# Attention step of a fused kernel: both halves of the next step's scores in one stretch, the mask moved to the end of the step before

## The chip, the cores and the metric

The kernel runs on one core of a Trainium2 chip. The metric is device time in microseconds of one execution; three runs of the kernel before gave a median of 325.79 us (325.31 to 326.69). The trace is of one more, profiled execution.

## The reference, cut to what matters

Three layers run one after another: a linear attention with decay, a mixture of experts with routing that carries over from token to token, and a gated convolution. Only the first is touched. In it, for each block of positions and each head:

```
intra = einsum('bhic,bhjc->bhij', qb, kb) * Dmask[None]      # scores, then mask
intra = einsum('bhij,bhjd->bhid', intra, vb)
inter = einsum('bhid,bhde->bhie', qb * lam_pow[None], kv_state)
out[:, :, sl] = intra + inter
kv_state = lam_block[None, :, None, None] * kv_state + einsum('bhsd,bhse->bhde', kb_dec, vb)
```

The attention's output `x` is then routed: the expert of a token is `argmax(x @ w_gate)` or, where a local gate says so, the expert of the token before; the softmax of the same logits scales the expert's answer.

## The kernel before, in words

The 1536 tokens (2 sequences of 768) are cut into 12 blocks of 128; each is handled for all 8 heads at once. All engines' instructions stand in the order in which the code is written: the whole attention part lies under `tc.manual_schedule` (L526 to L527), so each engine works its own list from first to last, and an instruction that waits holds up all behind it on that engine.

A loop over steps `s` (L553) is a software pipeline over three blocks: at step `s` block `s` gets its mask and scaled queries and keys, block `g1 = s-1` its attention output, block `g2 = s-2` its routing, and block `g3 = s-3` the last parts of routing. The pieces that the prediction follows, with the names of their tiles:

- `scores(g, half)` (L288, matmuls L300): query times key on TensorE, two head pairs to a half, into PSUM tiles `ps`. Its matmuls use 64 rows of the array; most neighbours use 128.
- `mask(g)` (L303, L307): two VectorE multiplications of `ps` by the decay mask, 128x512 each, into `sm`, which `mix(g)` reads (L326, TensorE, into `po`) one step later.
- `mixed(g1)` (L332): ScalarE copies `po` to `xt`; `turned(g1)` (L375, L378, L380): TensorE turns `xt` into token rows and logits, into PSUM tile `rt`.
- `logits(g2)` (L385) and `choice(g2)` (L419 to L421): VectorE takes the maximum `mx` of the logits in `rt`, its index, and the gate `fk`. From `mx` ScalarE makes `nmx` (`shift`, L404), `ex` (`exponents`, L409; it waits for VectorE's L420 as well), then `den` and the copies `xtok` (L391, L393), `softmax(g3)` (L429), then `xt` (L332) and `kp` (`kept`, L440). `kp` waits also for TensorE's `choice_turned` (L436), which reads `fk`.
- `experts(g2)` (L444): VectorE's scan over the tokens, from `kp` into `o_all`; then `keep_state(g1)` (L364, `state`), and at the step's end `keys_rest(s)` (L284, `kd`) and `first_lo` (L202, `wlo`, a weight's low part; from step 4 on). `experts_turned(g2)` (L448) on TensorE waits for `o_all`, and the program makes it wait for `state` too.

Blocks 5 and 11 end a sequence: `keys_rest` is left out at steps 5 and 11, `keep_state` at step 6, since no state follows them.

Of the kernel before, what the change touches and what calls it, by code (L numbers as in the profile page):

```python
# [44 lines left out]
def fused_kernel(ctx, tc, qkv, lam, wgl, w1, w2, wv, cw, wo, out, dbg=None):  # L45
# [148 lines left out]
    def split_hi(w, cs=slice(0, 1024)):  # L194
        if len(w) == 1:
            w.append(w4([P, 1024], F32R, "whi"))
        nc.scalar.copy(w[1][:, cs], w[0][:, cs])  # L197
# [51 lines left out]
    def first(n):  # L249
        return (w1_t if n < 4 else w2_t)[0][n % 4]  # L250

    def first_hi(n, cs=slice(0, 1024)):
        split_hi(first(n), cs)
# [16 lines left out]
    def key_tile(g):  # L270
        if g not in kd_t:
            kd_t[g] = at_p.tile([P, H, D], F32, name="kd", tag="kd")
        return kd_t[g]

    def keys(g, hs=range(HK)):

        if g % NC < NC - 1:
            kd = key_tile(g)
            for h in hs:
                nc.scalar.activation(kd[:, h, :], qk_t[g, 1][:, 0, h * D:(h + 1) * D], AF.Copy, scale=dm[:, h, P - 1:P])  # L280

    def keys_rest(g):
        if g % NC < NC - 1:
            nc.vector.tensor_tensor(  # L284
                key_tile(g)[:, HK:H], qk_t[g, 1][:, 0, HK * D:].rearrange("p (h d) -> p h d", h=H - HK),
                dm[:, HK:H, P - 1:P].to_broadcast([P, H - HK, D]), op=MUL)

    def scores(g, half, early=False):  # L288
        t = qk_t[g, 0]

        if half == 0 and early:
            rt = ps_1.tile([P, 2, HP, P], F32, name="rt", tag="rt")
            ps_t[g] = [rt[:, rh] for rh in range(2)]
        elif half == 0:
            ps_t[g] = [ps_s.tile([P, HP, P], F32, name=f"ps{rh}", tag=f"ps{rh}") for rh in range(2)]
        for hp in (2 * half, 2 * half + 1):
            for rh in range(2):
                r = slice(rh * 64, rh * 64 + 64)
                c0 = (hp % 2) * P
                nc.tensor.matmul(ps_t[g][rh][:, hp, :], t[r, half, 256 + c0:256 + c0 + P], t[r, half, c0:c0 + P],  # L300
                                 start=True, stop=True)

    def mask(g):  # L303
        ps = ps_t.pop(g)
        sm_t[g] = at_p.tile([P, 2, HP, P], F32, name="sm", tag="sm")
        for rh in range(2):
            nc.vector.tensor_tensor(sm_t[g][:, rh], ps[rh], dm[:, rh * HP:(rh + 1) * HP, :], op=MUL)  # L307
# [22 lines left out]
    def mixed(g):  # L330
        xt_t[g] = xt = at_p.tile([P, KD, P], F32, name="xt", tag="xt")
        nc.scalar.copy(xt.rearrange("p (j b) n -> p j b n", b=2),  # L332
                       po_t.pop(g)[:, :, 0:2 * P].rearrange("p b (j n) -> p j b n", j=2))
# [35 lines left out]
    def turned(g, ks=range(KD)):  # L369
        if 0 in ks:  # L370
            rv_t[g] = ps_1.tile([P, 2, 512], F32, name="rt", tag="rt")
        xt, rt = xt_t[g], rv_t[g]
        for k in ks:
            if k < 2:
                nc.tensor.matmul(rt[:, 0, k * P:k * P + XL], xt[:, k, :], wid[:, k, :], start=(k == 0), stop=False,  # L375
                                 skip_group_check=True)
            else:
                nc.tensor.matmul(rt[:, 0, P:XL], xt[:, k, :], wgl_sb[:, k, :], start=False, stop=(k == KD - 1),  # L378
                                 skip_group_check=True)
                nc.tensor.transpose(rt[:, 1, (k - 2) * P:(k - 1) * P], xt[:, k, :], ident)  # L380
# [21 lines left out]
    def shift(g):  # L402
        nmx_t[g] = nmx = at_p.tile([P, 1], F32, name="nmx", tag="nmx")
        nc.scalar.mul(nmx, lg_t[g][1][:, 0:1], -1.0)  # L404
# [117 lines left out]
    def warm(n):  # L522
        for _ in range(n):
            nc.tensor.matmul(pidx, warm_sb[:, 0:P], warm_sb, start=True, stop=True, skip_group_check=True)

    order_a = {mybir.EngineType.PE, mybir.EngineType.DVE, mybir.EngineType.Activation, mybir.EngineType.Pool, mybir.EngineType.SP}  # L526
    with tc.manual_schedule(engines=order_a):  # L527
        warm(10)
        scores(0, 0)
        scores(0, 1)  # L530
        warm(6)
        mask(0)
        keys(0)
        load_qk(3)
        load_qk(4)
        scores(1, 0, True)
        scores(1, 1, True)
        mix_state(0)
        mix(0, 0)
        mix(0, 1)  # L540
        mixed(0)
        mask(1)
        keys_rest(0)
        powers()
        next_state(0)
        warm(2)
        keep_state(0)
        queries(1)
        keys(1)
        keys_rest(1)  # L550
        scores(2, 0)
        turned(0)
        for s in range(2, NT):  # L553
            g1, g2, g3 = s - 1, s - 2, s - 3
            last = s == NT - 1
            if s < NT - 3:
                load_qk(s + 3)
            if s in (2, 4, 6, 8):
                load_next()
            if s in (9, 10):  # L560
                load_next(2)
            scores(s, 1)
            logits(g2)
            choice(g2)
            if last:
                ranks(g3)
                index_factors(g3)
            mask(s)
            decay(g1)
            shift(g2)  # L570
            exponents(g2)
            token_rows(g2)
            if 0 <= g3 < ET - 1:
                softmax(g3)
            if g3 >= 0 and not last:
                ranks(g3)
                index_factors(g3)
            mix_state(g1)
            mix(g1, 0)
            mix(g1, 1)  # L580
            mixed(g1)
            if last:
                counted_rest(g3)
                indices(g3)
                early_fetch()
            next_state(g1)
            choice_turned(g2, g1)
            inverse(g2)
            queries(s)
            kept(g2)  # L590
            if 3 <= s < 11:
                first_hi((s - 3) // 2, HALF[(s - 3) % 2])
            keys(s, range(2))
            experts(g2)
            keep_state(g1)
            if not last:
                scores(s + 1, 0)
            turned(g1, (0, 1))
            if last:
                turned(g1, (2, 3))  # L600
            experts_turned(g2)
            if not last:
                turned(g1, (2, 3))
            if last:
                softmax(g2)
                parts_hi(g2)
                first_hi(4, HALF[0])
            one_hots(g2)
            if last:
                first_hi(4, HALF[1])  # L610
            keys_rest(s)
            keys(s, range(2, HK))
            if s == NT - 2:
                softmax(g2)
            if s >= 4:
                first_lo((s - 4) // 2, HALF[s % 2])
            if g3 >= 0 and not last:
                counted_rest(g3)
                indices(g3)
            counted(g2)  # L620

        ge, g0, g1 = NT - 3, NT - 2, NT - 1
        logits(g0)
        choice(g0)
        shift(g0)
        exponents(g0)
        token_rows(g0)
        mix_state(g1)
        mix(g1, 0)
        mix(g1, 1)  # L630
        ranks(ge)
        places(ge)
        parts_lo(ge)
        mixed(g1)
        choice_turned(g0, g1)
        kept(g0)
        place(ge, (0,))
        first_lo(4, HALF[0])
        experts(g0)
        inverse(g0)  # L640
        parts_hi(g0)
        turned(g1, (0, 1))
        experts_turned(g0)
        turned(g1, (2, 3))
        one_hots(g0)
        counted_rest(ge)
        counted(g0)
        softmax(g0)
        load_next(4)
        load64(0)  # L650
        first_lo(4, HALF[1])
        place(ge, (1,))
        logits(g1)
        choice(g1)
        token_rows(g1)
        ranks(g0)
        places(g0)
        early_turn(0, (0, 1))
        choice_turned(g1, NT)
        early_turn(0, (2, 3))  # L660
        kept(g1)
        parts_hi(g1)
        experts(g1)
        parts_lo(g0)
        place(g0, (0,))
        experts_turned(g1)
        one_hots(g1)
        shift(g1)
        exponents(g1)
        counted_rest(g0)  # L670
        counted(g1)
        place(g0, (1,))
        ranks(g1)
        places(g1)
        inverse(g1)
        softmax(g1)
        parts_lo(g1)
        early_turn(1, (0, 1, 2, 3))
        place(g1)
        early_split()  # L680
        index_factors(ge)
        index_factors(g0)
        index_factors(g1)
# [3 lines left out]
    last = keep.tile([P, 2], F32, name="last")  # L687
# [657 lines left out]
```

## Time and profile before

| what | value |
|---|---|
| median of 3 runs | 325.79 us |
| the profiled execution's own time | 326.86 us |
| its span, first to last instruction | 325.1 us |
| attention: start of step 2's scores to the first expert matmul | 13.25 to 73.67 us of the span |
| TensorE busy, whole span | 315.7 us, 97% |
| VectorE, ScalarE busy, whole span | 259.0 us (80%), 208.6 us (64%) |
| granted TensorE clock, mean of the span | 0.997 |

PE is TensorE's matmuls, PEld its weight loads, DVE VectorE, ACT ScalarE. The matmuls' ends are modelled, and they overlap; what a group costs its engine is read from start to start. The same holds for VectorE and ScalarE, where an instruction's start lies a little before the end of the one ahead. An execution's time is the span and what lies around it.

### The profile page before, as it was taken

How to read it: one execution, taken by the hardware profiler on the slowest of the kernel's cores; microseconds unless marked ns; L12 is line 12 of the kernel's file. 1: busy time of each engine (PE TensorE's matmuls, PEld its weight loads, DVE VectorE, ACT ScalarE, POOL GpSimd, SP SyncE). 2: the span in 40 equal slices, each digit the busy share in tenths (PEclk: the TensorE clock that was granted, in tenths of full speed). 3: DMA queues.
4: the chain of work that ended last, by engine and by line, in shares of the span. 5: the costliest groups of instructions: out<-in, count | busy, mean ns of one | idle time of the engine just before them, and what ended most of it. 6: DMA issues, size and time to landing. Idle time of an engine off the chain costs nothing.

```text
span 325.1 us, 7326 instructions
## 1 busy us (share of the span) xinstructions
PE 315.7 (97%) x2722; PEld 277.2 (85%) x2722; DVE 259.0 (80%) x561; ACT 208.6 (64%) x518; POOL 91.5 (28%) x113
## 2 busy tenths in 40 slices
PE   8899999999999999999999999999999989999994
PEld 3688888789879899899798897988988969989984
DVE  5688899976958969959799798795845897977970
ACT  1589799966637756576567665864655774764641
POOL 7000000200445640541535405534332441020000
PEclk9999999999999999999999999999999999999998
DMA  7999899366679789589498697993303131331112
GB/s 213 390 389 310 289 375 323 131 209 242 197 251 374 299 287 357 216 315 351 171 343 346 193 398 300 314 386 112 102 34 111 36 98 69 100 94 66 66 42 95
DMA packets 27399, 73.09 MB, mean 225 GB/s; under 512 B 3798, under 2 KB 8156, under 8 KB 27356
## 3 DMA queue, kind: packets, MB, share of 16 engines
q1 hardware_dynamic: 24612, 64.83, 55.2%
q0 software_dynamic: 2304, 7.42, 7.4%
q8 instruction: 25, 0.41, 0.5%
q10 hardware_dynamic: 440, 0.30, 0.3%
q14 instruction: 18, 0.15, 0.1%
HBM read 57.79 MB, written 14.73 MB: 223 GB/s over the span
## 4 chain that ended last, share of the span: by engine, by line
PE 88%; DMA 5%; ACT 2%; DVE 2%; issue 1%; SPq 1%; POOL 0%; POOLq 0%; ACTq 0%
PE ph L854 27%; PE py L868 19%; PE py L1039 10%; PE pv L1013 7%; PE py L878 5%; PE ps L300 4%; PE po L326 3%; DMA qk<-in_qkv_dram 2%; PE rt L375 2%; PE po L318 2%; DMA yg<-ys,yslot 2%; DMA ys<-yo 1%; PE px L827 1%; PE sp L355 1%; PE rt L378 1%; PE rt L380 1%
## 5 line engine op out<-in xcount | busy, mean ns | idle before, releaser
L202 DVE TENSOR_TENSOR wlo<-wraw,whi 128x1024 fp32r<-128x1024 f32 (+1 forms) x69 | 83.4, 1235 | 12.9 <-ACT whi L197 12.9
L854 PE MATMUL ph<-xh,whi 128*128 128x240 f32 x512 | 87.0, 276 | 0.2 <-ACT xh L519 0.2
L854 PEld LDWEIGHTS ph<-xh,whi 128*128 128x128 f32 x512 | 77.4, 189 | 2.2 <-issue 1.2
L854 PE MATMUL ph<-xh,wlo 128*128 128x240 f32 x256 | 70.0, 275 | 0.0
L197 ACT CAST whi<-wraw 128x1024 fp32r<-128x1024 f32 (+1 forms) x69 | 65.6, 990 | 1.1 <-DVE wlo L202 1.0
L868 PE MATMUL py<-whi,hh 128*128 128x512 f32 x176 | 57.2, 396 | 0.0
L854 PEld LDWEIGHTS ph<-xh,wlo 128*128 128x128 f32 x256 | 48.5, 190 | 0.0
L999 DVE SCALAR_TENSOR_TENSOR gt<-yt,cw_sb,gt 128x256 f32<-128x256 f32 x96 | 39.0, 479 | 1.1 <-ACT gt L991 1.1
L868 PEld LDWEIGHTS py<-whi,hh 128*128 128x128 f32 x176 | 33.0, 188 | 7.4
L857 ACT ACTIVATE hh<-ph 128x480 fp32r<-128x480 f32 x32 | 18.3, 573 | 32.0 <-PE ph L854 31.7
L226 POOL TENSOR_TENSOR f64a<-f64a,f64s 128x512 f32<-128x512 f32 (+1 forms) x9 | 20.6, 2285 | 55.1 <-DVE f64s L225 55.0
L1013 PEld LDWEIGHTS pv<-yh,wv_t 128*128 128x128 f32 x288 | 35.2, 192 | 0.7 <-ACT gt L991 0.4
L1013 PE MATMUL pv<-yh,wv_t 128*128 128x256 f32 x288 | 35.7, 284 | 0.0
L868 PE MATMUL py<-wlo,hh 128*128 128x512 f32 x88 | 34.7, 395 | 0.0
L1039 PE MATMUL py<-wo_t,gh 128*128 128x512 f32 (+1 forms) x156 | 34.0, 375 | 0.0
L1039 PEld LDWEIGHTS py<-wo_t,gh 128*128 128x128 f32 x156 | 27.4, 188 | 5.0
L859 DVE SCALAR_TENSOR_TENSOR hh<-ph,hh 128x480 fp32r<-128x480 f32 x32 | 20.9, 653 | 9.3 <-ACT hf L858 9.3
L807 POOL DMA_INDIRECT xr<-xd,idx x14 | 19.6, 1398 | 9.9 <-DVE wlo L202 6.8
L957 POOL DMA_INDIRECT yg<-ys,yslot x8 | 11.4, 1422 | 30.2 <-PE pt L967 20.9
L868 PEld LDWEIGHTS py<-wlo,hh 128*128 128x128 f32 x88 | 16.5, 188 | 3.5
L878 PE MATMUL py<-wraw,hf 128*64 128x256 f32 x160 | 18.4, 382 | 0.0
L491 POOL DMA_INDIRECT xr<-xd,idx x2 | 2.1, 1054 | 52.0 <-ACT kp L440 51.7
(198 smaller groups left out, 520.2 us busy)
## 6 DMA issues: line engine op xcount, KB each, us to landing
wraw<-in_w_dram SPq DMA_DIRECT2D x64, 512.0 KB, 6.5
qk<-in_qkv_dram SPq DMA_DIRECT2D x23, 512.0 KB, 7.9
ys<-yo SPq DMA_DIRECT2D x16, 256.0 KB, 2.2
ys<-warm_sb SPq DMA_DIRECT2D x24, 128.0 KB, 1.9
xd<-xtok SPq DMA_DIRECT2D x11, 260.0 KB, 3.9
out_dram<-oo SPq DMA_DIRECT2D x11, 256.0 KB, 2.0
wraw<-in_w_val_dram SPq DMA_DIRECT2D x4, 512.0 KB, 8.3
wraw<-in_w_out_dram SPq DMA_DIRECT2D x4, 512.0 KB, 8.9
```

The costliest lines, as they stand in the source:

```text
L197: nc.scalar.copy(w[1][:, cs], w[0][:, cs])
L202: nc.vector.tensor_tensor(w[2][:, cs], w[0][:, cs], w[1][:, cs].bitcast(F32), op=SUB)
L226: nc.gpsimd.tensor_tensor(a.bitcast(F32), a.bitcast(F32), s.bitcast(F32), op=ADD)
L807: nc.gpsimd.indirect_dma_start(xr[:, t, :], None, xd, bass.IndirectOffsetOnAxis(ap=idx[:, 2 * e + t:2 * e + t + 1], axis=0))
L854: nc.tensor.matmul(ph[:, fi, :], w1_t[e][k][1 + a][:, f * P:(f + 1) * P], xh[b][:, k].rearrange("p t n -> p (t n)")[:, 0:C1], start=first, ...
L857: nc.scalar.activation(hh[:, 0, :, 0:C1], ph, AF.Relu)
L859: nc.vector.scalar_tensor_tensor(hh[:, 1, :, 0:C1], ph, 0.0, hh[:, 0, :, 0:C1].bitcast(F32), op0=ALU.max, op1=SUB)
L868: nc.tensor.matmul(py, hhs[f // 2][:, a, f % 2, t * P:(t + 1) * P], w2_t[e][f // 2][1 + b][:, (f % 2) * DM:(f % 2 + 1) * DM], start=(n == ...
L878: nc.tensor.matmul(py[i * NW:(i + 1) * NW, 0:DM // 2], hf[:, f, :], w2_t[e][f // 2][0][:, (f % 2) * DM + i * DM // 2:(f % 2) * DM + (i + 1 ...
L999: nc.vector.scalar_tensor_tensor(gt[:, k, :], yt_t[b, k][:, c0 + j:c0 + j + 256], cw_sb[:, k, j:j + 1], gt[:, k, :], op0=MUL, op1=ADD)
L1013: nc.tensor.matmul(pv[:, mi, :], wv_t[:, a, k * DM + m * P:k * DM + (m + 1) * P], yh[b][:, k, :], start=first, stop=last)
L1039: nc.tensor.matmul(po, gh[a][:, k, t * P:(t + 1) * P], wo_t[:, b, k * DM + cs.start:k * DM + cs.stop], start=(i == 0), stop=(i == 11))
```

## The change

The second half of `scores` no longer stands at the start of step `s` but behind the first half, at the end of the step before; eight short matmuls follow each other where four stood twice. `mask(s)` no longer stands behind `choice(g2)` in step `s` but as `mask(s+1)` at the end of step `s`, after `one_hots(g2)` and ahead of `keys_rest(s)` and `keys(s, ...)`. The first of them goes ahead of the loop. No instruction is added or removed, and none on ScalarE, GpSimd or the DMA queues changes its place.

```diff
--- before.py
+++ after.py
@@ -549,7 +549,9 @@
         keys(1)
         keys_rest(1)
         scores(2, 0)
+        scores(2, 1)
         turned(0)
+        mask(2)
         for s in range(2, NT):
             g1, g2, g3 = s - 1, s - 2, s - 3
             last = s == NT - 1
@@ -559,13 +561,11 @@
                 load_next()
             if s in (9, 10):
                 load_next(2)
-            scores(s, 1)
             logits(g2)
             choice(g2)
             if last:
                 ranks(g3)
                 index_factors(g3)
-            mask(s)
             decay(g1)
             shift(g2)
             exponents(g2)
@@ -595,6 +595,7 @@
             keep_state(g1)
             if not last:
                 scores(s + 1, 0)
+                scores(s + 1, 1)
             turned(g1, (0, 1))
             if last:
                 turned(g1, (2, 3))
@@ -608,6 +609,8 @@
             one_hots(g2)
             if last:
                 first_hi(4, HALF[1])
+            if not last:
+                mask(s + 1)
             keys_rest(s)
             keys(s, range(2, HK))
             if s == NT - 2:
```

VectorE, the end of step 8 and the start of step 9, before (the number behind a name is the tile's, `ps_958` the scores of block 9; `mx` belongs to block 7):

```order
L444 SCALAR_TENSOR_TENSOR o_all<-kp,sp 8x128
L364 TENSOR_TENSOR state<-sdec,sp 128x256
L284 TENSOR_TENSOR kd<-qk_598,dm 128x256
L202 TENSOR_TENSOR wlo<-wraw,whi 128x512
L385 MAX mx<-rt 128x8
L419 MAX_INDEX mi<-mx,rt 128x8
L420 TENSOR_SCALAR fk_136<-rt,thr 128x8
L421 SCALAR_TENSOR_TENSOR fk_136<-iota_133,mi,fk_136 128x8
L307 TENSOR_TENSOR sm<-ps_958,dm 128x512
L307 TENSOR_TENSOR sm<-ps_959,dm 128x512
L467 SCALAR_TENSOR_TENSOR scr,rk<-pidx,soall 128x8
```

and of the changed kernel, the same stretch:

```order
L444 SCALAR_TENSOR_TENSOR o_all<-kp,sp 8x128
L364 TENSOR_TENSOR state<-sdec,sp 128x256
L307 TENSOR_TENSOR sm<-ps_958,dm 128x512
L307 TENSOR_TENSOR sm<-ps_959,dm 128x512
L284 TENSOR_TENSOR kd<-qk_605,dm 128x256
L202 TENSOR_TENSOR wlo<-wraw,whi 128x512
L385 MAX mx<-rt 128x8
L419 MAX_INDEX mi<-mx,rt 128x8
L420 TENSOR_SCALAR fk_136<-rt,thr 128x8
L421 SCALAR_TENSOR_TENSOR fk_136<-iota_133,mi,fk_136 128x8
L467 SCALAR_TENSOR_TENSOR scr,rk<-pidx,soall 128x8
```

The two rows `sm` for block 9 stood behind `fk`; now they stand between `state` and `kd`, ahead of `mx`.

TensorE, the end of step 9 from the second row of `choice_turned` on, before (`ps_1064` are the scores of block 10):

```order
L436 MATMUL sp<-ident_100,fk_136 64x128
L300 MATMUL ps_1064<-qk_785 128x128
L300 MATMUL ps_1065<-qk_785 128x128
L300 MATMUL ps_1064<-qk_785 128x128
L300 MATMUL ps_1065<-qk_785 128x128
L375 MATMUL rt<-wid,xt 128x137 x2
L448 LDWEIGHTS o_all
L448 MATMUL sp<-ident_100,o_all 128x8
```

and of the changed kernel:

```order
L436 MATMUL sp<-ident_100,fk_136 64x128
L300 MATMUL ps_1064<-qk_792 128x128
L300 MATMUL ps_1065<-qk_792 128x128
L300 MATMUL ps_1064<-qk_792 128x128
L300 MATMUL ps_1065<-qk_792 128x128
L300 MATMUL ps_1064<-qk_792 128x128
L300 MATMUL ps_1065<-qk_792 128x128
L300 MATMUL ps_1064<-qk_792 128x128
L300 MATMUL ps_1065<-qk_792 128x128
L375 MATMUL rt<-wid,xt 128x137 x2
L448 LDWEIGHTS o_all
L448 MATMUL sp<-ident_100,o_all 128x8
```

The second four rows L300 of block 10 came after `turned` and the counting matmuls L460, ahead of L318; now they follow the first four at once.

## Rows read from the trace of the kernel before

**Rows 1.** The page, part 4: share of the chain that ended last, by engine.

```profile
PE 88%; DMA 5%; ACT 2%; DVE 2%; issue 1%; SPq 1%; POOL 0%; POOLq 0%; ACTq 0%
```

**Rows 2.** Windows; busy time (instructions) of each engine, granted clock, DMA share, GB/s.

```profile
9.00:13.25 4.25, 3.55 (x50) 2.72 (x51) 2.95 (x8) 2.59 (x9) 0.33 (x2) 1.00 0.99 391
52.23:57.21 4.98, 4.98 (x83) 4.32 (x85) 4.69 (x17) 4.83 (x22) 0.00 (x0) 1.00 0.84 292
28.04:62.47 34.43, 34.17 (x539) 29.57 (x539) 31.73 (x110) 31.34 (x138) 0.00 (x0) 1.00 0.84 297
```

**Rows 3.** Timeline of ScalarE; start us, us, engine, line, op, out<-in.

```profile
28.04 0.26 ACT L440 ACTIVATE kp<-sp 8x128 f32<-8x128 f32 x1
...
37.88 0.26 ACT L440 ACTIVATE kp<-sp 8x128 f32<-8x128 f32 x1
...
41.97 0.26 ACT L440 ACTIVATE kp<-sp 8x128 f32<-8x128 f32 x1
...
47.29 0.26 ACT L440 ACTIVATE kp<-sp 8x128 f32<-8x128 f32 x1
...
52.23 0.26 ACT L440 ACTIVATE kp<-sp 8x128 f32<-8x128 f32 x1
...
55.30 0.20 ACT L404 ACTIVATE nmx<-mx 128x1 f32<-128x1 f32 x1
55.53 0.27 ACT L409 ACTIVATE ex<-rt,nmx 128x8 f32<-128x8 f32 x1
...
56.75 0.58 ACT L332 COPY xt<-po 128x512 f32<-128x512 f32 x1
57.21 0.26 ACT L440 ACTIVATE kp<-sp 8x128 f32<-8x128 f32 x1
...
62.47 0.27 ACT L440 ACTIVATE kp<-sp 8x128 f32<-8x128 f32 x1
```

**Rows 4.** Timeline of VectorE, steps 9 and 10.

```profile
52.53 0.47 DVE L444 TENSOR_TENSOR_SCAN o_all<-kp,o_all,sp 8x128 f16<-8x128 f32 x1 [0.17 <-ACT kp L440]
52.92 0.38 DVE L364 TENSOR_TENSOR state<-sdec,sp 128x256 f32<-128x256 f32 x1
53.24 0.40 DVE L284 TENSOR_TENSOR kd<-qk,dm 128x256 f32<-128x256 f32 x1
53.57 0.67 DVE L202 TENSOR_TENSOR wlo<-wraw,whi 128x512 fp32r<-128x512 f32 x1
54.26 0.17 DVE L385 MAX8 mx<-rt 128x8 f32<-128x8 f32 x1
...
55.01 1.28 DVE L307 TENSOR_TENSOR sm<-ps,dm 128x512 f32<-128x512 f32 x2
56.21 0.16 DVE L467 SCALAR_TENSOR_TENSOR scr<-pidx,soall 128x8 f32<-128x8 f32 x1
```

**Rows 5.** Timeline of all engines, one place where `ex` waited.

```profile
39.59 0.17 DVE L385 MAX8 mx<-rt 128x8 f32<-128x8 f32 x1
...
39.96 0.21 DVE L420 TENSOR_SCALAR fk<-rt,thr 128x8 f16<-128x8 f32 x1
...
40.29 0.27 ACT L409 ACTIVATE ex<-rt,nmx 128x8 f32<-128x8 f32 x1 [0.28 <-PE ps L300]
```

**Rows 6.** Timeline of TensorE, three places.

```profile
9.09 1.16 PE L300 MATMUL rt<-qk 64*128 64x128 f32 x16 [0.85 <-DMA qk<-in_qkv_dram]
...
29.94 0.17 PE L460 MATMUL pidx<-so,upto 128*128 128x8 f16 x1
30.03 0.71 PE L300 MATMUL ps<-qk 64*128 64x128 f32 x8
30.68 0.67 PE L318 MATMUL po<-qs,state 64*64 64x128 f32 x16
...
64.07 0.17 PE L460 MATMUL pidx<-so,upto 128*128 128x8 f16 x1 [0.28 <-ACT soall L454]
64.17 0.67 PE L318 MATMUL po<-qs,state 64*64 64x128 f32 x16
```

## The prediction

> **What bounds the kernel now.** I read the page's chain of waits first: 88% of it is TensorE [rows 1]. That speaks for a matmul-bound kernel, but it is a share of the whole span, and the change lies in the attention steps alone. So next I read one full step by windows, from one `kp` on ScalarE to the next, 52.23 to 57.21: 4.98 us, in which TensorE is busy 4.98, ScalarE 4.83 and VectorE 4.69 us, at a granted clock of 1.00 [rows 2]. Three engines are within 6% of the step, so no one of them can be sped up alone, and what counts is how they wait for each other. The stretch that the change can lengthen runs from `kp` of step 4 at 28.04 to `kp` of step 11 at 62.47, 34.43 us in seven intervals [rows 3].
>
> The wait that matters is a ring through ScalarE and VectorE. I put it together from the timelines of both, start to start. On VectorE the maximum `mx` comes first. On ScalarE `nmx` and `ex` follow it, then, in order, the copies to `xtok`, `xt` and `kp`. VectorE's scan `o_all` waits for `kp`; behind it in VectorE's list stand `state`, `kd`, `wlo`, and then the next `mx`. Because each engine works its list in order, the next `mx` can't start until the scan of this step is done, and the next `kp` not until that `mx` is. Before the change it takes:
> - `mx` to `ex` where `ex` waited: 39.59 to 40.29, 0.70 us. The trace puts that wait down to scores; the program has `ex` wait for VectorE's L420 too, which ends at 39.96 + 0.21 = 40.17, and I take that [rows 5].
> - `ex` to `kp`, 55.53 to 57.21: 1.68 [rows 3].
> - `kp` to `o_all`, 52.23 to 52.53: 0.30 [rows 3, 4].
> - `o_all` to `state` 0.39, `state` to `kd` 0.32, `kd` to `wlo` 0.33 [rows 4].
> - `wlo` to `mx`: 0.69 as the rows stand, but `mx` waited there for TensorE. The two mask instructions have the size of `wlo`, and their pair takes 1.28 with a second one of about 0.68, so a follower starts after 0.60 [rows 4]. I take 0.60; with 0.69 a turn is 0.09 longer.
>
> Sum: 0.70 + 1.68 + 0.30 + 0.39 + 0.32 + 0.33 + 0.60 = 4.32 us, 0.66 below the step of 4.98. So the ring is slack now.
>
> **The change part by part.** *The mask.* Two instructions that cost VectorE 1.20 us from start to start, 55.01 to 56.21 [rows 4]. They stood behind `fk`, after `mx`: outside the ring, while ScalarE did its 1.68 us of copies. Now they stand between `state` and `kd`, ahead of the next `mx`: inside the ring. VectorE has no more work, and its wait for `kp` gets longer by what was taken from there. The ring becomes 4.32 + 1.20 = 5.52 us, over the step by 0.54. What is queued behind the mask: `kd`, `wlo`, `mx`, and through `mx` ScalarE's `nmx` and all behind it; through `xt` and `kp` TensorE's `turned` (L375) and, by `o_all` and `state`, L448. The mask's own wait, for the second half of the scores, costs nothing: those matmuls now follow `choice_turned` and are done about when `kp` starts, and the mask comes 0.30 + 0.39 + 0.32 = 1.01 us after it.
>
> Seven intervals, `kp` to `kp`, from step 4 to step 11:
> - five with all pieces (from steps 4, 7, 8, 9, 10): 5 x 5.52 = 27.60;
> - from step 5 `kd` is left out: 5.52 - 0.33 = 5.19; from step 6 `state` is left out: 5.52 - 0.32 = 5.20.
>
> Together 37.99 against 34.43 [rows 3]: +3.56 us. The largest single gain in length is from step 6 to 7, now 41.97 - 37.88 = 4.09. In steps 2 and 3 there is no `wlo`, the ring is 4.92 and just slack: no loss; I take no gain there either, since ScalarE sets the pace with 4.83 busy, and bound it by 0.6 (three times the 0.19 below). After step 11 no mask is left in either kernel, and the rest moves back as one piece: +3.56.
>
> *The scores.* The same eight program matmuls, in one stretch. A separate second stretch costs, from the start of L460 to that of L318, 30.68 - 29.94 = 0.74. Where L318 follows L460 directly it is 64.17 - 64.07 = 0.10. Sixteen records in one stretch take 1.16 and eight 0.71, so the longer stretch adds 0.45. Saved: 0.74 - 0.10 - 0.45 = 0.19 us of TensorE a step [rows 6]. It is hidden: TensorE, with 4.79 of work in 5.52, now waits in each step, for `xt` before L375 and for `state` before L448. If that cover were gone, it would be the gain of the second case below.
>
> The Trainium skill, Perfetto Trace Analysis, section on identifying the most-contended engine, says to take the engine with the highest occupancy and to optimize it first. By that, TensorE with 4.98 of 4.98 would be the one, and 0.19 a step would come off. No run here shows it yet; the ring speaks against it.
>
> *DMA and the rest.* The second half needs no transfer that the first doesn't need, since both read one tile. No queue has its list changed.
>
> The profiled execution took 326.86 us, 1.76 more than its span of 325.1: the sum gives 326.9 + 3.6 = 330.4 for it. It lies 1.07 above the median of the runs, 325.79, and carried to that the forecast is 329.4.
>
> **Rivals.**
> 1. *The ring binds*, as above: 329.4. Its own range is 328.2 to 330.6: below by 0.6 for gains in steps 2 to 4 and as much again for one interval less; above by 0.09 a turn and by up to 0.6 for ScalarE's two extra copies of indices in step 11.
> 2. *TensorE was the bound and gets faster.* Mechanism: ten separate stretches vanish, at 0.19 each, 1.9 us: 323.9. It decides if every other chain, the ring among them, is under 4.79 a step. For it: TensorE's share of the chain. Against it: ScalarE alone is busy 4.83, and the ring sums to 5.52.
> 3. *No change.* VectorE's work fits in the step (4.69 of 4.98), so moving it within the step costs nothing: 325.8, or 325.2 with a little of the gain. It holds if the ring's slack is 1.20 or more, where I read 0.66. Against it: each term is a difference of two starts.
> 4. *The clock.* TensorE's waits in each step could bring its granted clock from 2.4 to 1.2 GHz. Then its 4.79 us a step would double at most, 4.06 over the ring's 5.52 in seven steps: some 28 us more, 358. Against it: from 9.00 to 13.25 it was busy 3.55 of 4.25, 84%, and the clock stood at 1.00 [rows 2]; 4.79 of 5.52 is 87%.
>
> **How the numbers follow.** The first case has 0.86, the second 0.04, the third 0.08, the fourth 0.02. The likeliest gives 329.4. For the range I widen its own: to 327.6, where only half of the 3.56 shows, and to 331.0, where each of the seven turns is longer by 0.2 than the sum of its terms. What a measurement of this kernel can tell from no change is 0.5%, 1.6 us: slower is above 327.4, faster below 324.2. Slower: the first and fourth case, and a little less for a ring that binds in a few steps only, 0.87. Faster: 0.04. Same: 0.09.
>
> **What would show it.** In the profile of the changed kernel, `kp` to `kp` should be 5.5 us from step 7 to 10 and 5.2 from steps 5 and 6, and the first 28 us nearly as before. `nmx` should wait for `mx` in each of those steps, and `o_all` for `kp` by about 0.7. TensorE's rows L375 and L448 should wait some 0.4 us each for `xt` and `state`, though its scores take less. The expert matmuls should start about 3.6 us later, and all after them be as long as before. If `kp` to `kp` stays at 4.98, the ring was misread, and above all the price of `ex` to `kp`; if it falls to 4.8, TensorE was the bound.

## The result, and the profile after

The changed kernel took 329.09 us (median of 19 runs, 327.36 to 332.16), the kernel before 325.76 in 19 runs beside it. The ratio is 1.0103 [1.0082, 1.0124], which is 3.36 us more (2.67 to 4.04): slower by more than the 0.5% that a measurement can tell. The forecast was 329.4.

The page's chain of waits, by engine, of the changed kernel; it answers to [rows 1]:

```profile
PE 81%; DMA 7%; ACT 6%; DVE 3%; issue 0%; ACTq 0%
```

TensorE's share fell from 88% to 81%, and ScalarE and VectorE, 2% each before, have 9% together. That alone says only where to look. The windows of the changed kernel, step 8 and then all from `kp` of step 4 to `kp` of step 11 (columns as in [rows 2]):

```profile
50.53:55.97 5.44, 4.96 (x81) 4.28 (x81) 4.66 (x16) 4.94 (x23) 0.00 (x0) 1.00 0.84 297
29.22:66.89 37.67, 33.51 (x524) 28.38 (x522) 31.69 (x109) 31.64 (x139) 0.00 (x0) 1.00 0.76 258
```

The step is 5.44 us instead of 4.98, and TensorE is busy in 4.96 of it: no engine fills the step any more, at a granted clock of 1.00. So the engines wait for each other. Who waits for whom stands in the waits of the changed kernel from 13 to 66 us (engine, line, what it waited for: us in total, times, longest):

```profile
DVE o_all L444 <- ACT kp L440: 5.8, 9, 1.2
ACT nmx L404 <- DVE mx L385: 4.2, 7, 1.4
PEld rt L375 <- ACT xt L332: 3.4, 7, 0.5
PEld L448 <- DVE state L364: 2.5, 6, 0.4
```

ScalarE waits for VectorE's maximum, VectorE for ScalarE's `kp`, and TensorE for both. That is a ring, and TensorE stands outside of it. Its turns are read from ScalarE's timeline of the changed kernel, which answers to [rows 3] (start us, us, engine, line, op, out<-in, in brackets the idle time before and its releaser):

```profile
18.07 0.27 ACT L440 ACTIVATE kp<-sp 8x128 f32<-8x128 f32 x1
...
19.86 0.17 ACT L453 CAST so<-sp 128x8 f16<-128x8 f32 x1 [1.05 <-PE sp L448]
...
23.49 0.26 ACT L440 ACTIVATE kp<-sp 8x128 f32<-8x128 f32 x1
24.60 0.62 ACT L197 CAST whi<-wraw 128x512 fp32r<-128x512 f32 x1 [0.85 <-DMA wraw<-in_w_dram]
...
29.22 0.26 ACT L440 ACTIVATE kp<-sp 8x128 f32<-8x128 f32 x1
...
34.71 0.26 ACT L440 ACTIVATE kp<-sp 8x128 f32<-8x128 f32 x1
...
38.19 0.27 ACT L409 ACTIVATE ex<-rt,nmx 128x8 f32<-128x8 f32 x1 [0.28 <-DVE fk L420]
...
39.87 0.26 ACT L440 ACTIVATE kp<-sp 8x128 f32<-8x128 f32 x1
...
45.04 0.26 ACT L440 ACTIVATE kp<-sp 8x128 f32<-8x128 f32 x1
...
50.53 0.26 ACT L440 ACTIVATE kp<-sp 8x128 f32<-8x128 f32 x1
...
54.28 0.27 ACT L409 ACTIVATE ex<-rt,nmx 128x8 f32<-128x8 f32 x1 [0.28 <-PE po L326]
...
55.97 0.26 ACT L440 ACTIVATE kp<-sp 8x128 f32<-8x128 f32 x1
...
61.46 0.26 ACT L440 ACTIVATE kp<-sp 8x128 f32<-8x128 f32 x1
...
65.28 0.27 ACT L409 ACTIVATE ex<-rt,nmx 128x8 f32<-128x8 f32 x1 [0.28 <-PE po L326]
...
66.89 0.26 ACT L440 ACTIVATE kp<-sp 8x128 f32<-8x128 f32 x1
```

From `kp` to `kp` it is 5.42 (step 2 to 3) and 5.73 (to step 4), and then, from step 4 at 29.22 to step 11 at 66.89, 5.49, 5.16, 5.17, 5.49, 5.44, 5.49 and 5.43. VectorE's timeline of the changed kernel, one turn, answers to [rows 4]:

```profile
50.83 0.41 DVE L444 TENSOR_TENSOR_SCAN o_all<-kp,sp 8x128 f16<-8x128 f32 x1 [0.60 <-ACT kp L440]
51.16 0.38 DVE L364 TENSOR_TENSOR state<-sdec,sp 128x256 f32<-128x256 f32 x1
...
53.61 0.15 DVE L385 MAX8 mx<-rt 128x8 f32<-128x8 f32 x1
...
56.26 0.47 DVE L444 TENSOR_TENSOR_SCAN o_all<-kp,o_all,sp 8x128 f16<-8x128 f32 x1 [0.60 <-ACT kp L440]
56.66 0.38 DVE L364 TENSOR_TENSOR state<-sdec,sp 128x256 f32<-128x256 f32 x1
56.97 1.27 DVE L307 TENSOR_TENSOR sm<-ps,dm 128x512 f32<-128x512 f32 x2
58.17 0.40 DVE L284 TENSOR_TENSOR kd<-qk,dm 128x256 f32<-128x256 f32 x1
58.50 0.67 DVE L202 TENSOR_TENSOR wlo<-wraw,whi 128x512 fp32r<-128x512 f32 x1
59.11 0.15 DVE L385 MAX8 mx<-rt 128x8 f32<-128x8 f32 x1
```

The mask's pair `sm` now stands between `state` and `kd`, ahead of `mx`. The turn from `mx` to `mx`, start to start: `mx` to `ex` 0.67, `ex` to `kp` 1.69, `kp` to `o_all` 0.29, to `state` 0.40, to `sm` 0.31, to `kd` 1.20, to `wlo` 0.33, to `mx` 0.61. The sum is 5.50 us, and the turn itself is 59.11 - 53.61 = 5.50. The row at 54.28 puts the 0.28 that `ex` waited down to TensorE's `po`, which would bring TensorE into the ring. But at 38.19 `ex` has the same wait, put down to VectorE's L420, and starts while those matmuls of `po` (37.31, 1.09 long) still run; `mx` starts at 37.52 there, so `mx` to `ex` is the same 0.67. It is L420 that `ex` waits for, as the prediction took it. TensorE's timeline of the changed kernel in the same turn answers to [rows 6]:

```profile
54.66 1.16 PE L300 MATMUL ps<-qk 64*128 64x128 f32 x16
56.14 0.74 PE L375 MATMUL rt<-wid,xt 128*128 128x137 f32 x4 [0.31 <-ACT xt L332]
57.10 0.18 PE L448 MATMUL sp<-ident,o_all 128*128 128x8 f16 x1 [0.23 <-DVE state L364]
...
57.87 0.17 PE L460 MATMUL pidx<-so,upto 128*128 128x8 f16 x1
57.97 0.45 PE L318 MATMUL po<-qs,state 64*64 64x128 f32 x8
```

All sixteen score records stand in one stretch, and L318 follows L460 after 0.10, as it did before only where no scores lay between them. TensorE waits for `xt` before L375 and for `state` before L448.

**Where the time went, between the two profiled spans.** They are 325.1 and 327.8 us, 2.70 apart. `kp` of step 2 starts at 18.08 before and 18.07 after. From there to `kp` of step 4 the changed kernel loses 1.19 (11.15 against 9.96): 0.45 from step 2 to 3, and 0.74 from step 3 to 4, where ScalarE waits 0.85 us at 24.60 for a weight's transfer, the row of L197 above. From step 4 to 11 it loses 37.67 - 34.43 = 3.24. From there to the first expert matmul both take the same, 11.25 and 11.20; that matmul starts at 78.14 against 73.67. Behind it the changed kernel is 1.77 shorter, of which 1.53 is one wait of the kernel before for a gather. Its row in the trace of before:

```profile
262.30 0.52 PE L967 MATMUL pt<-identr,yg 128*128 128x128 f32 x4 [1.53 <-DMA yg<-ys,yslot]
```

Neither of the two transfer waits belongs to the change: the repeat of the changed kernel (`e8_again`, below) lacks the first and has the second, with 1.5 us.

### The profile page after: what moved, and what is told of

Same layout as the page of the kernel before. It is cut to its first block, busy times and chain, and to the rows that moved or that the text cites. A ratio compares the mean times of both kernels' runs of the same rounds, so it can differ in the third digit from the quotient of the medians.

```text
span 327.8 us, 7334 instructions
## 1 busy us (share of the span) xinstructions
PE 315.4 (96%) x2722; PEld 276.7 (84%) x2722; DVE 260.3 (79%) x561; ACT 208.5 (64%) x518; POOL 89.6 (27%) x113
## 4 chain that ended last, share of the span: by engine, by line
PE 81%; DMA 7%; ACT 6%; DVE 3%; issue 0%; ACTq 0%
PE ph L857 27%; PE py L871 19%; PE pv L1016 11%; PE py L1042 10%; PE py L881 5%; DMA wraw<-in_w_dram 3%; DMA qk<-in_qkv_dram 3%; PE po L326 2%; PE px L830 1%; ACT xt L332 1%; PE po L318 1%; DMA lam_sb<-in_lam_dram 1%; DVE o_all L444 1%; PE pt L970 1%; ACT ex L409 1%; PE px L511 1%
## 5 line engine op out<-in xcount | busy, mean ns | idle before, releaser
L202 DVE TENSOR_TENSOR wlo<-wraw,whi 128x1024 fp32r<-128x1024 f32 (+1 forms) x69 | 84.5, 1251 | 12.9 <-ACT whi L197 12.9
L197 ACT CAST whi<-wraw 128x1024 fp32r<-128x1024 f32 (+1 forms) x69 | 65.5, 990 | 1.9 <-DVE wlo L202 1.0
L226 POOL TENSOR_TENSOR f64a<-f64a,f64s 128x512 f32<-128x512 f32 (+1 forms) x9 | 18.3, 2033 | 55.1 <-DVE f64s L225 55.0
L810 POOL DMA_INDIRECT xr<-xd,idx x14 | 20.6, 1473 | 8.8 <-DVE wlo L202 5.8
L960 POOL DMA_INDIRECT yg<-ys,yslot x8 | 9.5, 1188 | 30.3 <-PE pt L970 21.1
L491 POOL DMA_INDIRECT xr<-xd,idx x2 | 2.1, 1054 | 56.3 <-ACT kp L440 56.0
```

The source lines that it names most:

```text
L202: nc.vector.tensor_tensor(w[2][:, cs], w[0][:, cs], w[1][:, cs].bitcast(F32), op=SUB)
L226: nc.gpsimd.tensor_tensor(a.bitcast(F32), a.bitcast(F32), s.bitcast(F32), op=ADD)
L810: nc.gpsimd.indirect_dma_start(xr[:, t, :], None, xd, bass.IndirectOffsetOnAxis(ap=idx[:, 2 * e + t:2 * e + t + 1], axis=0))
```

## The experiments

Eight runs were made, seven of new kernels and one of the changed kernel again, in two groups of four, each group on one chip with the kernel before beside it (325.89 us in the first group, 326.63 in the second). Ratios are to that.

**One half of the change alone: the scores** (`e1_scores_only`). From the changed kernel, the mask put back behind `choice`:

```diff
-        mask(2)
         for s in range(2, NT):
...
             choice(g2)
+            mask(s)
             decay(g1)
...
-            if not last:
-                mask(s + 1)
```

> Both halves of the scores in one stretch, as in the changed kernel; the mask back behind the gate fk, where it stood before. Ring theory: the mask is out of the ring again, which sums to 4.32 us under a step of 4.98 us that ScalarE sets, so TensorE's saved 0.19 us a step hides: 325.8 us, 325.0 to 326.5 us, no change within 0.3%; kp to kp 4.98 in full steps. If it is the longer stretch of scores that costs (it delays the turning of xt by 0.45 us in each step): some +3.3 us, 329 us. If TensorE were the bound and gained: ten times 0.19, 323.9 us.

Measured: 326.0 us, ratio 1.0019 [0.9992, 1.0045], no difference that can be told. With the mask outside of the ring the loss is gone. The window of this kernel from `kp` of step 8 to that of step 9:

```profile
47.73:52.64 4.91, 4.88 (x87) 4.26 (x85) 4.65 (x17) 4.82 (x23) 0.00 (x0) 1.00 0.96 351
```

From step 4 to 11 it takes 34.35 against 34.43. So what the merge saves TensorE came to 0.08 us in seven steps of this trace, not to 7 x 0.19. One loss remains, from step 2 to 3: 5.48 against 4.97. The timeline of this kernel at the start of that interval:

```profile
17.78 1.23 PE L300 MATMUL ps<-qk 64*128 64x128 f32 x16
...
18.94 0.74 PE L375 MATMUL rt<-wid,xt 128*128 128x137 f32 x4
...
19.75 0.17 ACT L453 CAST so<-sp 128x8 f16<-128x8 f32 x1 [1.12 <-PE sp L448]
```

TensorE is late at this point. The longer stretch (1.23 at 17.78, where before eight records took 0.71 from 17.97) holds up L375 and L448 behind it, and ScalarE's `so` (L453) waits 1.12 us for L448, where it waited 0.60 in the timeline of the kernel before:

```profile
19.43 0.17 ACT L453 CAST so<-sp 128x8 f16<-128x8 f32 x1 [0.60 <-PE sp L448]
```

**The other half alone: a mask ahead of `mx`** (`e2_mask_only`). From the kernel before:

```diff
             scores(s, 1)
+            mask(s)
             logits(g2)
             choice(g2)
-            mask(s)
```

> The mask ahead of the maximum mx, the scores left in two stretches. Ring theory: the mask is in the ring, and with it TensorE, since the mask must now wait for the second half of the scores that follows turned and the counting matmuls. kp to L448 1.1 us, to the second half 0.86, its matmuls 0.72, mask 1.20, mx to ex 0.70, ex to kp 1.68: 6.1 to 6.3 us a step against 4.98; over nine to ten steps +10 to +13 us, 336 to 339 us. If the place of the mask does not matter: 325.8 us. If only the mask's own 1.20 us counts, as in the changed kernel: 329 us.

Measured: 339.49 us, 1.0438 [1.0385, 1.0491]; the ring theory's direction, a little above its numbers (336 to 339 us, 6.1 to 6.3 us a step). From step 3 to 5 `kp` starts at 25.45, 31.77 and 38.08, which is 6.32 and 6.31 to a turn. That is more than the mask's 1.20 on the 4.32 of before, since the mask here waits inside the ring for scores that are issued just ahead of it. The timeline of this kernel in step 4:

```profile
33.10 0.67 DVE L202 TENSOR_TENSOR wlo<-wraw,whi 128x512 fp32r<-128x512 f32 x1
...
33.76 0.71 PE L300 MATMUL ps<-qk 64*128 64x128 f32 x8
...
34.51 1.29 DVE L307 TENSOR_TENSOR sm<-ps,dm 128x512 f32<-128x512 f32 x2 [0.73 <-PE ps L300]
...
35.71 0.17 DVE L385 MAX8 mx<-rt 128x8 f32<-128x8 f32 x1
...
35.91 0.20 ACT L404 ACTIVATE nmx<-mx 128x1 f32<-128x1 f32 x1 [0.98 <-DVE mx L385]
```

From `wlo` to `sm` it takes 1.41, of which 0.60 is `wlo`'s own and 0.81 the wait for the scores; then come 1.20 for the mask, and only then `mx`, for which ScalarE waited 0.98. So 4.32 + 0.81 + 1.20 = 6.33 against 6.31. Two later intervals were longer, 6.90 (step 5 to 6) and 6.50 (step 8 to 9); there the clock had fallen, as the last section shows. So this run shows the mask's place and the sum of its turn; its total time has the clock in it as well.

**Half of the mask in the ring** (`e3_half_mask`). From the changed kernel, `mask` split into its two instructions:

```diff
             choice(g2)
+            mask(s, 1)
             decay(g1)
...
             if not last:
-                mask(s + 1)
+                mask(s + 1, 0)
```

> The changed kernel with one of the two mask instructions at the end of the step before and the other behind fk. Ring theory: the ring is 4.32 + 0.60 = 4.92 us, just under the step of 4.98, so nothing shows: 325.9 us, 325.2 to 326.7 us, kp to kp 4.98. If each mask instruction ahead of mx has its price by itself: half of the change, +1.7 us, 327.4 us.

Measured: 325.49 us, 0.9998 [0.9969, 1.0026]. The ring is 5.50 - 0.60 = 4.90 in a full turn, and the steps from 4 and 9 took 4.97. From step 8 to 9, where the scan is shorter, the ring is 5.44 - 0.60 = 4.84 and the step took 4.91, in which TensorE is busy 4.88 and ScalarE 4.82; the window of this kernel:

```profile
46.63:51.54 4.91, 4.88 (x87) 4.27 (x85) 4.56 (x17) 4.82 (x22) 0.00 (x0) 1.00 0.94 326
```

With one half in the ring nothing is lost, with both the whole 1%. That is how a ring with slack behaves: here it lies 0.07 below the step's other limits and is free, in the changed kernel it lies above them and sets the step.

**The mask left at the end, another 0.60 us taken out of the ring** (`e4_lo_outside`). From the changed kernel:

```diff
             choice(g2)
+            if s >= 5:
+                first_lo((s - 5) // 2, HALF[(s - 1) % 2])
             decay(g1)
...
-            if s >= 4:
+            if last:
                 first_lo((s - 4) // 2, HALF[s % 2])
```

> The changed kernel with the mask where the change puts it, at the end of the step, but the weight's low part wlo (0.60 us) moved from there to behind fk of the next step. Ring theory: what counts is the sum of what stands between the scan o_all and mx, 5.52 - 0.60 = 4.92 us, under 4.98: 325.9 us, 325.2 to 326.8 us, though the mask is where it was put. If the mask's place itself costs (what it waits for, or the traffic with TensorE's PSUM there): 329 us as the change.

Measured: 325.48 us, 1.0000 [0.9973, 1.0026]; step 4 to 11 took 34.06. VectorE's timeline of this kernel:

```profile
46.80 0.67 DVE L267 TENSOR_TENSOR qs<-qk,lq 128x512 f32<-128x512 f32 x1
47.72 0.41 DVE L444 TENSOR_TENSOR_SCAN o_all<-kp,sp 8x128 f16<-8x128 f32 x1 [0.25 <-ACT kp L440]
...
48.37 1.27 DVE L307 TENSOR_TENSOR sm<-ps,dm 128x512 f32<-128x512 f32 x2
49.57 0.40 DVE L284 TENSOR_TENSOR kd<-qk,dm 128x256 f32<-128x256 f32 x1
49.90 0.15 DVE L385 MAX8 mx<-rt 128x8 f32<-128x8 f32 x1
...
50.64 0.68 DVE L202 TENSOR_TENSOR wlo<-wraw,whi 128x512 fp32r<-128x512 f32 x1
```

The mask `sm` stands where the change put it and takes as long, and the time is that of before, since `wlo` now lies behind `mx`. So it isn't the mask's place as such that costs, nor the merged scores; it is the sum between `kp` and `mx`.

**ScalarE eased, with and without the change** (`e5_scores_pool`, `e6_before_pool`, `e7_after_pool`). In all three the second pair of `kd`, two ScalarE activations (L280, 0.59 us together), becomes one GpSimd multiplication; e5 has it on top of e1, e6 on the kernel before, e7 on the changed kernel:

```diff
+    def keys_pool(g):
+        if g % NC < NC - 1:
+            nc.gpsimd.tensor_tensor(
+                key_tile(g)[:, 2:HK], qk_t[g, 1][:, 0, 2 * D:HK * D].rearrange("p (h d) -> p h d", h=HK - 2),
+                dm[:, 2:HK, P - 1:P].to_broadcast([P, HK - 2, D]), op=MUL)
...
-            keys(s, range(2, HK))
+            keys_pool(s)
```

> As the run with merged scores and the mask behind fk, and in each step the second pair of ScalarE's kd multiplications (two of 0.24 us, one pair a step) done by GpSimd as one 128x128 multiplication. Theory: ScalarE set the pace with 4.83 us busy of 4.98; without 0.48 of it the next bound is TensorE, whose step the merged scores cut to 4.79, so 0.19 us a step over some ten steps shows, and a little of the waits on state with it: 323.5 to 324.2 us, -1.7 to -2.3 us. If ScalarE did not set the pace: 325.8 us, no change. If GpSimd's work slows VectorE: slower than 325.8 us.

> The kernel before with the same two kd multiplications a step on GpSimd, scores in two stretches. Theory: TensorE's step of 4.9 to 4.98 us is next after ScalarE's, so only the short waits of TensorE on state go: 324.8 to 325.5 us, -0.3 to -1.0 us. If ScalarE alone set the pace, with TensorE far behind: as much as with merged scores, -2 us.

> The changed kernel with the same two kd multiplications a step on GpSimd. Ring theory: they are not in the ring (they stand between kp and the next nmx, where ScalarE waits for mx anyway), so 5.52 us a step stays: 328.8 to 329.4 us, as the change. If the change is slow because ScalarE has too much to do: back to 326 us or less.

Measured: e5 324.86 us, 0.9959 [0.9925, 0.9993]; e6 325.93, 0.9991 [0.9955, 1.0027]; e7 329.49, 1.0105 [1.0071, 1.0139]. What speaks for the ring is e7: ScalarE was relieved of 0.48 us a step and the step stayed. Its window from step 8 to 9:

```profile
48.93:54.36 5.43, 4.96 (x81) 4.28 (x81) 4.65 (x16) 4.46 (x20) 0.70 (x1) 1.00 0.83 293
```

It is 5.43 against 5.44 us with ScalarE at 4.46 instead of 4.94. That pair of `kd` is not between `mx` and `kp`, so it has no part in the turn. The kernel e5 has the lowest ratio of all, 1.3 us (0.2 to 2.4) below the kernel before. That is less than the 0.5% named in the prediction, and less than the 1.7 to 2.3 us that were expected, though the interval reaches that far. For e6 the interval holds both no change and the 0.3 to 1.0 us that were expected. Neither step alone did it: e1 left ScalarE with 4.82 in a step of 4.91, and in e6 TensorE was busy 4.91 of 4.91. Whether e5 beats e6 the intervals leave open. From step 4 to 11 the traces have 33.91 for e5, 34.30 for e6 and 34.35 for e1; e3 and e4, with ScalarE's list as it was, have 34.04 and 34.06.

**The changed kernel again** (`e8_again`), the same code:

> The changed kernel once more, unchanged, for a second trace. Theory: kp to kp 5.4 to 5.5 us in full steps again, 329 us; the 0.85 us for which whi waited for its weight's transfer in the first trace, and with it the 1.2 us by which kp of step 4 was late, is the chance of one execution and differs this time. If the change itself makes that transfer late, whi waits again by 0.5 us or more.

Measured: 330.51 us, 1.0101 [1.0037, 1.0165], and from step 4 to 11 37.62 us. Step 3 to 4 took 4.96 here, without the 0.85 us wait for a weight; step 2 to 3 took 5.42 again.

## Why the prediction was right

**The ring: right, and shown.** It was summed as 5.52 us and measured as 5.50 in one turn; full steps took 5.43 to 5.49, those without `kd` or `state` 5.16 and 5.17 (forecast 5.19 and 5.20). The seven intervals made 37.67 and 37.62 us in two traces, 37.99 forecast, so +3.24 and not +3.56. Every term is within 0.03 of its price. `mx` to `ex`, 0.67 instead of 0.70, takes 0.03 from each turn; in step 8, where the second sequence begins, the scan is 0.07 shorter (50.83 to 51.16 above), and `ex` to `kp` of step 11 took 1.61 (65.28 to 66.89). These make 7 x 0.03 + 0.07 + 0.07 = 0.35, about the 0.32 by which the sum was too high. What was said to show it is there: `o_all` waits 0.60 for `kp` in a full step (0.7 forecast), `nmx` waits for `mx` in six of the seven intervals (the table's seventh wait, of 1.4, lies ahead of step 2), by 0.16 in full steps; L375 and L448 wait 0.31 and 0.23 for `xt` and `state`, where some 0.4 was forecast. That the ring is the cause, and not the move as such, is shown by taking 0.60 us out of it in two ways (e3, e4: no loss) and by relieving ScalarE beside it (e7: the whole loss stays).

**The slack of 0.66: borne out.** e3 and e4 put 0.60 of net work into the ring, less than the slack that was read, and neither cost time that can be told; e2 and the changed kernel put more into it, and both did. How far above 0.60 it reaches no run shows.

**The scores: right that the gain is hidden.** TensorE's stretch is what the sum had (1.16 for sixteen records, L318 0.10 after L460), and in the changed kernel the gain is lost in waits of 0.31 and 0.23 on TensorE. In e1, without the mask in the ring, still only 0.08 us came off in seven steps. That ScalarE with 4.82 is next there is argued, and e5, where it was relieved too, speaks for it only in part. There 0.44 more came off, between step 9 and step 11 (9.59 against 10.05); between step 5 and step 8 nothing did (14.46 against 14.42), while e3 and e4, with ScalarE's list as in e1 and half of the mask or `wlo` elsewhere on VectorE, took 14.10 there. So VectorE's list seems to hold up those steps; no run tests that by itself. The forecast 4.79 us of TensorE work a step is not what the windows count as busy, 4.88 in e1's step and 4.96 in the changed kernel's.

**Steps 2 and 3: wrong.** The sum had "no loss". From step 2 to 3 the changed kernel lost 0.45 us, in both of its traces, and e1, which shares only the merged scores with it, took 5.48 there (e3 and e4 5.41 and 5.42). The step that failed is that the longer stretch of scores was priced only as work that TensorE saves, and not as a delay to what stands behind it. In step 2 TensorE runs late, and 0.45 more ahead of L375 goes straight to `so` on ScalarE, whose wait went from 0.60 to 1.05 us (the rows of L453 above). From `so` to `kp` ScalarE then takes as long as before, 19.86 to 23.49, 3.63, against 19.43 to 23.05, 3.62; so the delay reached `kp` through ScalarE's list. Where `kd`'s second pair is off that list, the interval is 5.00 with the merge (e5, e7) and 4.83 without it (e6): most of the delay is gone, not all. "The first 28 us nearly as before" was wrong by this 0.45; the 0.74 that the profiled execution lost on top of it is the wait for the weight. In sum the steps cost 3.24 + 0.45 = 3.69 us, against 3.56 forecast and 3.36 (2.67 to 4.04) measured: two errors of size, 0.32 too much and 0.45 too little, nearly cancelled. That 329.4 came within 0.3 us of 329.09 is in part luck. One sum of the prediction is off as well: seven turns longer by 0.2 each give 329.4 + 1.4 = 330.8, where the range was ended at 331.0; nothing rests on it.

**The DMA and all after step 11: right, with scatter.** From step 11 to the first expert matmul it is 11.25 against 11.20. Single transfer waits of 0.85 and 1.53 us come and go from one execution to the next, and each is a quarter or more of the effect; hence +2.70 from the two spans alone.

**The rivals.** TensorE as the bound (323.9) fell with e1: the merge alone gains nothing that can be told. The rule cited from the Trainium skill, Perfetto Trace Analysis, Identifying the Most-Contended Engine, names the engine with the highest occupancy as the one to optimize first; for TensorE, it adds, headroom is judged by the matmuls' arithmetic (MFU) and the busy share of the weight loads, which the prediction left out. The weight loads are busy 4.32 of 4.98 [rows 2], less than ScalarE's 4.83, so with that addition the 4.98 does not make TensorE the one to begin with. Neither engine relieved alone, TensorE in e1 or ScalarE in e6, gave a gain that can be told. The loss of the changed kernel came from the order on VectorE, the least busy of the three. No change (325.8) fell with the ratio itself. The clock held: 1.00 in the stretch of the changed kernel, though TensorE was idle for 0.48 us of a step.

## What to carry to other kernels

Where three engines each fill over 90% of a loop's step, sum the loop's rings of waits from start to start, and ask of each moved instruction whether it goes into one: VectorE did the same work before and after, and 1.20 us of it moved by a few rows cost 0.5 us in each step, because the price is what is put in less the slack. Work belongs behind the instruction that another engine waits for; and a merge that shortens an engine's sum still delays what stands right behind the longer stretch.

## What the runs showed of the hardware that was not expected

**The clock fell in a step with a thin stretch.** In e2, windows of this kernel (columns as in [rows 2]):

```profile
31.00:32.00 1.00, 0.24 (x5) 0.06 (x1) 0.46 (x1) 1.00 (x5) 0.00 (x0) 1.00 0.43 172
37.00:38.00 1.00, 0.49 (x8) 0.29 (x6) 0.75 (x2) 1.00 (x4) 0.00 (x0) 1.00 0.12 41
40.00:41.00 1.00, 1.00 (x13) 0.98 (x11) 0.00 (x0) 0.00 (x0) 0.00 (x0) 0.50 1.25 397
```

TensorE was busy 0.49 us from 37 to 38, 0.73 and 0.79 in the next two, and from 40 to 41, when it was busy throughout, the granted clock was 0.50, which is 1.2 of 2.4 GHz; from step 8 to 9 (50.98 to 57.48) it averaged 0.74. One thin microsecond alone did not do it: from 31 to 32 TensorE was busy only 0.24, and from 32 to 37 the clock stayed at 1.00. What decides between the two places stays open. The eight score records that start at 40.15 took 1.23 us, against 0.71 in the timeline of step 4 above. The changed kernel, with waits of 0.2 and 0.3 us on TensorE in a step, stayed at 1.00. So the fourth rival was not empty: it came with a turn of 6.3 us, not of 5.5.

**GpSimd's multiplication slowed VectorE's.** In e5 the new instruction ran beside `qs`; the timeline of this kernel:

```profile
46.77 0.40 POOL L290 TENSOR_TENSOR kd<-qk,dm 128x128 f32<-128x128 f32 x1 [4.94 <-PE sp L442]
46.83 0.89 DVE L267 TENSOR_TENSOR qs<-qk,lq 128x512 f32<-128x512 f32 x1
```

VectorE's 128x512 multiplication took 0.89 us there and 0.67 alone (the row at 46.80 in e4's timeline): 0.22 more, beside 0.40 us of GpSimd, 0.34 of which lay within it. It goes both ways: in step 2 of e5 `qs` started first, at 17.43, and took its 0.67, and GpSimd's multiplication, from 17.60 on, took 0.76 instead of 0.40. In e5 VectorE's busy time in the step from 46.88 to 51.78 was 4.78 of 4.90 us, against 4.65 of 4.91 in e1. That this is a part of why e5 gained only 1.3 us is likely and was not tested by itself.
